# A Fourier mixer and a two-layer network on one core: transform tables in thirds, and another order of loads at the start

## The chip, the cores and the metric

The kernel runs on 1 core of one Trainium2 chip. The metric is the device time of one execution in microseconds (us), as the median of several runs. Only one core works, so its own span is the whole story. The engines are named as in the profile: PE (matrix products; PEld is its weight loading), DVE (vector), ACT (activation), POOL (GpSimd, which here only issues transfers) and SP (which also only issues transfers).

## The reference

Eight sequences of 3,008 rows and 256 columns are filtered in the frequency domain along the rows, and every row of the result goes through two dense layers with a PReLU between them. Inputs and output are float32.

```python
X = np.fft.rfft(x, axis=1)                       # x: (8, 3008, 256)
Y = X * (filt_r + 1j * filt_i)[None, :, :]       # 1505 frequencies x 256
y = np.fft.irfft(Y, n=3008, axis=1).reshape(24064, 256)
h = y @ w_in                                     # (24064, 2048)
g = np.maximum(h, 0.0) + alpha * np.minimum(h, 0.0)
out = g @ w_out                                  # (24064, 256)
```

## The kernel before

**The transform.** A transform of 3,008 = 94 x 32 points is done as matrix products: a product with a 94-point table (`wf1` or `wfx`), a reordering, a product with the twiddle table `twf`, the multiplication with the filter, a product with the inverse twiddle tables `twi` (and `twx`, for batch 0), another reordering and a product with `wi3`. Its result is the transposed activation `yT` in fp16. A twiddle table has 24 entries along its middle dimension, two for each of the 12 steps `kp` of batch 0; they can be loaded in slices such as 0:8, 8:16 and 16:24.

**Batch 0** (class `First`) has nothing to overlap with, so it is a prologue of its own, written out in order. `piece_a` (8 pieces) is the first product, `turn_at` transposes, `twice` copies a third of `twf` into a doubled form on ACT, `piece_b(kp)` is the second product followed by DVE's multiplication with the filter (line 304, output `uu`), `piece_c(kp)` is the inverse product with `twi` and `twx` (line 324, outputs named `op` or `psF`), and `keep_c` evicts it. `piece_b` writes one of two PSUM buffers called `hps`; DVE's multiplication frees it. The loop over `kp` runs `piece_b(kp + 2)`, then `piece_c(kp)`. The helper `warm` issues products whose result nobody reads.

**Loads of the prologue.** There are two queues, and each is in order. SP loads `id16`, `wfx`, the first third of `twf`, the first filter row `fst` (line 122), then at `i == 3` the rest of the tables and small constants (lines 365 and 392 to 396). GpSimd loads x of batch 0 (line 112, with conversion to fp16), filter rows 1 to 4, 4 to 8 and 8 to 12 (line 122, eight transfers each), then at `kp == 5` the layer weights `win_s` and `wout_s` (lines 422 and 424) and x of batch 1, and at last the copy of `fst` into `filt_s` (line 431) and copies within the filter (434, 436). A small `memset` by DVE into the target stands ahead of some loads: the load must wait for it, so it starts no sooner than DVE gets there. Each queue has eight completion semaphores in turn, so that a transfer also waits for the landing of the one eight places ahead of it.

**Buffers that couple things.** `fst` and `asb` (the evicted first product of batches 1 to 7, line 255 with output `asb`) have one buffer together: asb of batch 1 cannot be written before the copy of `fst` has been made. x has four buffers (`p_x`), one for each quarter of a batch.

**The main loop.** The rows go through the two layers in 48 blocks of 512 (now and then 384) rows with 16 steps each; a step is a product with `w_in` (`up`, line 481, output `hps`), ACT's eviction into `gtb` (line 490), DVE's PReLU (493 and 495), and the product with `w_out` of the block before (`down`, line 512, output `op`). The transforms of batches 1 to 7 are spread over these steps by `plan_fft`, whose arguments are step numbers: `a_at` for the first product (line 155), `x_at` for the loads of the next batch's x, `b_at` for the second product (line 179) with DVE's two multiplications (186 and 187) and the swap of partitions by transfers `uu<-ww` (line 191, GpSimd's queue), `c_at` for the inverse product (line 210). For batch 1 `b_at` is 36, 42, ..., 66 and `c_at` is 48, 54, ..., 78. For batch 2 the loads of the x that follows are at steps 57, 69, 81 and 89.

Of the kernel before, what the change touches and what calls it, by code (L numbers as in the profile page):

```python
# [24 lines left out]
def _build_consts():  # L25

    n1, n2, p = np.arange(N1), np.arange(N2), np.arange(32)
    k1 = (2 * (np.arange(NK) // 2) + 24 * (np.arange(NK) % 2))[None, :] + np.arange(2)[:, None]
    k2 = np.where(p < 16, p, 47 - p)
    g = np.where(p < 16, 1.0, -1.0)  # L30

    a1 = 2 * np.pi * n1[:, None, None] * k1[None] / N1
    wf1 = np.stack([np.cos(a1), -np.sin(a1)], axis=2)
    scale = np.where((k1 == 0) | (k1 == 47), 1.0, 2.0)[None, :, None, :] / NFFT
    wi3 = (wf1 * scale).reshape(N1, 96).T
    wfx = wf1.transpose(0, 3, 1, 2).reshape(N1, 96)
    wf1 = wf1.reshape(N1, 96)

    kk = k1[:, :, None] + N1 * k2
    ang = 2 * np.pi * n2[:, None, None, None] * kk[None] / NFFT  # L40
    c, s = np.cos(ang), np.sin(ang)
    fwd = np.array([[c, -s * g], [s, c * g]])
    twf = fwd.transpose(3, 0, 2, 4, 1, 5).reshape(128, NK, 64)
    inv = np.array([[c, s], [-s * g, c * g]])
    inv = inv.reshape(2, 2, N2, 2, NK // 2, 2, 32).transpose(5, 0, 6, 4, 3, 1, 2)
    inx = np.stack([inv[:, 1], -inv[:, 0]], axis=1)
    return wf1, wfx, wi3, twf, inv.reshape(128, NK, 64), inx.reshape(128, NK, 64)
# [3 lines left out]
def kernel(  # L51
# [10 lines left out]
    nc = tc.nc  # L62
    names = ("wf1", "wfx", "wi3", "twf", "twi", "twx")
    consts = {n: nc.inline_tensor(np.ascontiguousarray(v).astype(np.float16), name="c_" + n)
              for n, v in zip(names, _build_consts())}
    sgn = np.tile(np.repeat([1.0, -1.0], 32), 2)[:, None].astype(np.float32)
    sgn_d = nc.inline_tensor(sgn, name="c_sgn")
    id32_d = nc.inline_tensor(np.eye(16, dtype=np.float32), name="c_id32")
# [17 lines left out]
    wf1_s = konst.tile([N1, 96], FP16, name="wf1_s")  # L86
    wfx_s = konst.tile([N1, 96], FP16, name="wfx_s")
    wi3_s = konst.tile([96, N1], FP16, name="wi3_s")
    twf_s = konst.tile([128, NK, 64], FP16, name="twf_s")
    twi_s = konst.tile([128, NK, 64], FP16, name="twi_s")  # L90
    filt_s = konst.tile([128, 12, 2, D], FP16, name="filt_s")
    filts_s = konst.tile([128, 12, 2, D], FP16, name="filts_s")
    al16 = konst.tile([16, 128], FP32, name="al16")
    id32 = konst.tile([16, 16], FP32, name="id32")
# [7 lines left out]
    sgn_s = konst.tile([128, 1], FP32, name="sgn_s")  # L102
    yT = konst.tile([128, 2, 2 * NFFT], FP16, name="yT")

    def xrow(b, c):
        return bass.AP(tensor=x.tensor, offset=x.offset + (b * NFFT + 8 * c) * D,
                       ap=[[N2 * D, N1], [1, 8 * D]])

    def load_x(b, c):
        xs = p_x.tile([N1, 8 * D], FP16, name="xs")  # L110
        for r in (slice(0, 48), slice(48, N1)) :
            nc.gpsimd.dma_start(out=xs[r], in_=xrow(b, c)[r])  # L112
        return xs

    def load_filt(eng, dst, ha, hb):
        n = hb - ha
        for i, src in enumerate((filt_r, filt_i)):
            for e in range(2):
                q = 64 * e + 32 * i
                k = 2 * ha + 24 * e  # L120
                for j, step, off in ((0, 1, k), (16, -1, N1 - k)):
                    eng.dma_start(
                        out=dst[q + j : q + j + 16, ha:hb].rearrange("p h r d -> p (h r) d"),
                        in_=bass.AP(tensor=src.tensor, offset=src.offset + off * D,
                                    ap=[[N1 * D, 16], [step * D, 2 * n], [1, D]]))

    def banks(wide):
        if wide:
            return psH.tile([128, 2, 512], FP32, name="hps")
        return psF.tile([128, 2, 512], FP32, name="psF")  # L130

    def bank(kind):
        if kind == "o":
            return psO.tile([128, 2, D], FP32, name="op").rearrange("p k d -> p (k d)")
        return banks(kind == "h")[:, 0]
# [226 lines left out]
    def tables(eng, names, ka, kb):  # L362
        for n, t in (("twf", twf_s), ("twi", twi_s), ("twx", twx_s)):
            if n in names:
                eng.dma_start(out=t[:, ka:kb], in_=consts[n].ap()[:, ka:kb])

    xc = {(0, c): load_x(0, c) for c in range(4)}
# [6 lines left out]
    def warm(n, pw):  # L374
        for _ in range(n):
            nc.tensor.matmul(pw.rearrange("p (r c) -> p r c", r=4), id16,  # L376
                             id16.unsqueeze(1).to_broadcast([128, 4, 128]), start=True, stop=True)

    warm(9, bank("o"))
    for i in range(8):  # L380
        f0.piece_a(i, both[i % 2], i % 3 < 2)
        if i % 2 == 1:
            warm((4, 4, 6, 3)[i // 2], bank("o"))
        if i == 1:
            nc.vector.memset(f0.fst[:, 0, :, 0:1], 0.0)
            load_filt(nc.sync, f0.fst, 0, 1)
        if i == 3:
            nc.vector.memset(twf_s[:, 8:24, 0:1], 0.0)
            tables(nc.sync, ("twf",), 8, 24)
            tables(nc.sync, ("twi", "twx"), 0, 8)  # L390
            tables(nc.sync, ("twi", "twx"), 8, 24)
            nc.sync.dma_start(out=wi3_s, in_=consts["wi3"].ap())
            nc.sync.dma_start(out=al16, in_=moe_alpha.rearrange("(j p) -> j p", p=128))
            nc.sync.dma_start(out=id32, in_=id32_d.ap())
            nc.sync.dma_start(out=wf1_s, in_=consts["wf1"].ap())
            nc.sync.dma_start(out=sgn_s, in_=sgn_d.ap())
        if i == 5:
            f0.twice(0, 8)
    f0.turn_at(0, 1, on_act)
    f0.turn_at(1, 1, on_dve, True)  # L400
    warm(2, bank("o"))
    f0.piece_b(0)
    f0.turn_at(2, 2, on_act)
    f0.twice(8, 16)
    f0.piece_b(1)
# [3 lines left out]
    for kp in range(12):  # L409
        if kp < 10:  # L410
            f0.piece_b(kp + 2)
        f0.piece_c(kp)
        if kp > 9:
            f0.keep_c(kp, (on_act, on_act) if kp == 10 else both, 1)
        elif kp % 2 == 1:
            f0.keep_c(kp - 1, (on_act, on_act))
            if kp < 7:
                f0.turn_at(kp + 5, 2, on_act)
        if kp == 5:
            nc.vector.memset(win_s[:, 0, 0:2], 0.0)  # L420
            for kt in range(2):
                nc.gpsimd.dma_start(out=win_s[:, kt], in_=moe_w_in[kt * 128 : (kt + 1) * 128])
            for q in range(2):
                nc.gpsimd.dma_start(
                    out=wout_s[:, 8 * q : 8 * q + 8],
                    in_=moe_w_out[1024 * q : 1024 * q + 1024].rearrange("(j p) d -> p j d", p=128))
            for c in range(4):
                xc[(1, c)] = load_x(1, c)
        if 7 <= kp < 10:
            warm(2, banks(False)[:, 0])  # L430
# [92 lines left out]
    def put(step, fn, *args):  # L523
        plan.setdefault(step, []).append((fn, args))

    def plan_fft(b, a_at, ta, quarters, x_at, b_at, add, c_at, d_at):
        f = Fft(b)
        for i in range(8):
            put(a_at[i], f.piece_a, i)
            front.add(a_at[i])  # L530
        for c in range(4):
            put(a_at[2 * c + 1], f.save_a, c)
            if b + 1 < NB:
                put(x_at[c],
                    lambda b=b, c=c: xc.update({(b + 1, c): load_x(b + 1, c)}))
        for q in range(quarters):
            w = NK // quarters
            put(ta, f.turn_a, nc.sync, w * q, w * q + w)
        for q in range(6):
            put(b_at[q], f.piece_b, q, not add)  # L540
            if add:
                put(b_at[q] + add, f.piece_s, q)
        for q in range(6):
            put(c_at[q], f.piece_c, q)
            front.add(c_at[q])
            if q % 2 == 1:
                put(c_at[q] + 1, f.turn_c, q // 2)
        for i in range(8):
            put(d_at[i], f.pair_d, i, on_act)
# [13 lines left out]
    def d_steps(p):  # L563
        return [p + t for t in (91, 93, 104, 108, 116, 120, 140, 152)]

    plan_fft(1, range(12, 28, 2), 28, 4, (34, 42, 54, 66), range(36, 72, 6), 0, range(48, 84, 6),
             (92, 94, 97, 100, 111, 121, 142, 154))
    plan_fft(2, (50, 56, 62, 68, 74, 80, 82, 84), 90, 4, (57, 69, 81, 89),
             (106, 116, 126, 136, 148, 158), 7, (116, 126, 136, 148, 158, 172), d_steps(96))
    for b in range(3, NB):  # L570
        p = 96 * (b - 1)
# [54 lines left out]
```

## Time and profile before

| | |
|---|---|
| median of 3 runs | 790.9 us (789.08 to 791.35) |
| the profiled execution | 787.85 us, its span 786.0 us |
| mean granted PE clock | 0.993 |
| PE busy | 769.7 us (98% of the span) |
| DVE, ACT busy | 595.5 us (76%), 587.0 us (75%) |
| chain that ended last | PE 92%, DMA 4% |
| transfers | 100.66 MB, SP's queue 34.1% and GpSimd's 21.5% of 16 engines |

The chain is the sequence of work, followed back from the last instruction, that set the end. A share of 98% for PE says that nearly all of the span is PE's, but not at which clock, and matrix products overlap, so that a busy PE is not one at its peak. The first 60 us, in which batch 0 is transformed and the loop fills, look otherwise than the rest: there PE waits, and there the granted clock is 0.50 in two stretches.

### The profile page before, as it was taken

The page shows a single profiled execution, that of the slowest core. Times are in us where ns is not written, and L with a number is a line of the kernel's source. Part 1 is how long each engine was busy: PE and PEld are TensorE (multiplying, and loading weights), DVE is VectorE, ACT ScalarE, POOL GpSimd, SP SyncE. Part 2 cuts the span into 40 slices and gives each one's busy share as a digit, 9 for nine tenths or more (in the row PEclk, how much of TensorE's full clock was granted, in tenths as well). Part 3 has the DMA queues.
Part 4 walks back from the last instruction along what each step waited for, and adds up shares of the span by engine and source line. Part 5 has one row for each costly group of instructions (what it writes and reads, how often), then busy time and mean ns, then how long its engine had stood idle before and what let it go on. Part 6 is the DMA issues. An engine that isn't in the chain of part 4 may idle for free.

```text
span 786.0 us, 16085 instructions
## 1 busy us (share of the span) xinstructions
PE 769.7 (98%) x6349; PEld 511.8 (65%) x6349; DVE 595.5 (76%) x1116; ACT 587.0 (75%) x673; POOL 142.7 (18%) x271
## 2 busy tenths in 40 slices
PE   7889999999999999999999999999999999999997
PEld 4547666666666666766666666766666666766665
DVE  3668885788868887788877888688877888766663
ACT  4578787887778887798777887788876777677663
POOL 6420471122202221122201222011200121000000
PEclk9899999999999999999999999999999999999999
DMA  9897698766754657455593655734474233511112
GB/s 188 133 180 203 125 185 181 234 136 161 144 156 109 146 136 148 135 123 126 128 216 73 148 124 130 189 82 108 109 154 129 57 86 93 147 38 28 42 41 55
DMA packets 95084, 100.66 MB, mean 128 GB/s; under 512 B 11280, under 2 KB 82464, under 8 KB 94816
## 3 DMA queue, kind: packets, MB, share of 16 engines
q1 hardware_dynamic: 80368, 70.25, 34.1%
q0 software_dynamic: 14640, 29.38, 21.5%
q8 instruction: 50, 0.82, 0.4%
q14 instruction: 26, 0.21, 0.1%
HBM read 55.28 MB, written 46.66 MB: 130 GB/s over the span
## 4 chain that ended last, share of the span: by engine, by line
PE 92%; DMA 4%; issue 1%; POOL 1%; ACT 1%; DVE 1%; POOLq 0%; ACTq 0%; DVEq 0%
PE op L512 41%; PE hps L481 41%; PE hps L155 3%; PE psF L232 3%; DMA filt_s<-in_filt_r_dram 2%; PE psF L179 2%; PE hps L210 1%; DMA uu<-ww 1%; DMA filt_s<-fst 1%; POOL xs L112 1%; PE psF L346 0%; PE op L324 0%; ACT gtb L490 0%; PE hps L299 0%; PE psF L376 0%
## 5 line engine op out<-in xcount | busy, mean ns | idle before, releaser
L490 ACT ACTIVATE gtb<-hps 128x1024 f16<-128x1024 f32 (+1 forms) x384 | 385.8, 1005 | 133.2 <-PE hps L481 132.3
L512 PE MATMUL op<-wout_s,gtb 128*128 128x256 f16 x3008 | 436.3, 273 | 0.1
L481 PE MATMUL hps<-yT,win_s 128*128 128x512 f16 (+1 forms) x1536 | 434.8, 375 | 1.2 <-ACT gtb L490 1.1
L512 PEld LDWEIGHTS <-gtb 128*128 128x128 f16 x3008 | 294.0, 98 | 168.9 <-issue 0.9
L493 DVE TENSOR_SCALAR m<-gtb,alm_s 128x512 f16<-128x512 f16 (+1 forms) x768 | 233.0, 346 | 150.7 <-ACT gtb L490 149.7
L495 DVE TENSOR_TENSOR gtb<-gtb,m 128x2048 f16<-128x2048 f16 (+1 forms) x192 | 231.0, 1203 | 10.4 <-PE hps L481 0.5
L481 PEld LDWEIGHTS <-win_s 128*128 128x128 f16 x1536 | 142.8, 98 | 61.5 <-issue 15.4
L193 POOL DMA_DIRECT2D sw<-ww x144 | 71.1, 501 | 380.7 <-DVE ww L186 377.8
L255 ACT ACTIVATE asb<-hps 96x1024 f16<-96x1024 f32 x56 | 57.1, 1020 | 13.1 <-PE hps L155 11.7
L517 ACT ACTIVATE osb<-op 128x512 f32<-128x512 f32 (+1 forms) x97 | 56.2, 579 | 5.3 <-issue 2.8
L255 ACT ACTIVATE v<-hps 128x1024 f16<-128x1024 f32 x42 | 43.0, 1025 | 15.7 <-PE hps L210 15.7
L112 POOL DMA_DIRECT2D xs<-in_x_dram x64 | 39.1, 700 | 85.6 <-PE hps L155 73.9
L255 ACT ACTIVATE yT<-psF 128x752 f16<-128x752 f32 x59 | 47.0, 797 | 7.8 <-PE psF L232 7.7
L186 DVE TENSOR_TENSOR ww<-psF,filts_s 128x1024 f16<-128x1024 f32 x42 | 51.1, 1218 | 0.0
L187 DVE TENSOR_TENSOR uu<-psF,filt_s 128x1024 f16<-128x1024 f32 x42 | 51.0, 1215 | 0.0
L155 PE MATMUL hps<-xs,wf_s 94*96 94x512 f16 x112 | 33.9, 384 | 1.4 <-ACT asb L255 1.4
L232 PE MATMUL psF<-wi_s,zt 96*128 96x94 f16 x500 | 31.2, 205 | 0.2
L232 PEld LDWEIGHTS <-zt 96*128 96x128 f16 x512 | 28.6, 98 | 2.9 <-issue 0.6
L191 POOL DMA_DIRECT2D uu<-ww x24 | 19.3, 1208 | 31.6 <-DVE uu L187 26.4
L198 DVE TENSOR_TENSOR uu<-uu,sw 128x1024 f16<-128x1024 f16 x36 | 24.7, 685 | 0.3 <-DMA sw<-ww 0.3
L210 PE MATMUL hps<-uu,twi_s 64*64 64x256 f16 x336 | 16.8, 271 | 1.1 <-DMA uu<-ww 1.1
L179 PE MATMUL psF<-at,twf_s 64*64 64x256 f16 x336 | 17.3, 281 | 0.0
(67 smaller groups left out, 173.2 us busy)
## 6 DMA issues: line engine op xcount, KB each, us to landing
out_dram<-osb SPq DMA_DIRECT2D x160, 128.0 KB
a_dram<-asb SPq DMA_DIRECT2D x28, 384.0 KB
v_dram<-v SPq DMA_DIRECT2D x84, 128.0 KB
zt<-v_dram SPq DMA_DIRECT2D x28, 384.0 KB
sw<-ww POOLq DMA_DIRECT2D x144, 64.0 KB, 2.4
at<-a_dram SPq DMA_DIRECT2D x20, 384.0 KB
xs<-in_x_dram POOLq DMA_DIRECT2D x32, 192.0 KB, 4.5
xs<-in_x_dram POOLq DMA_DIRECT2D x32, 184.0 KB, 5.8
```

Source lines behind the costliest of these rows:

```text
L155: nc.tensor.matmul(ps[0:96, u], wf1_s, xs[:, o : o + 512], start=True, stop=True)
L186: nc.vector.tensor_mul(ww, px, fs)
L187: nc.vector.tensor_mul(uu, px, f)
L193: nc.gpsimd.dma_start(out=sw[o : o + 32], in_=ww[i : i + 32])
L232: nc.tensor.matmul(ps[:, m], self.zt[:, 8 * g + 4 * mh + m, dh * 128 : dh * 128 + 128], wi3_s, start=True, stop=True)
L255: nc.scalar.activation(o, i, AF.Copy)
L481: nc.tensor.matmul(self.hps[:, j % 2, 0:tn], win_s[:, kt, j * 128 : (j + 1) * 128], yT[:, kt, self.t0 : self.t0 + tn], start=(kt == 0), st ...
L490: nc.scalar.activation(g[:, 2 * i : 2 * i + 2], self.hps[:, :, 0:tn], AF.Copy)
L493: nc.vector.tensor_scalar(m[:, 2 * i + h], g[:, 2 * i + h], 0.0, a, OP.min, OP.mult)
L495: nc.vector.tensor_add(g, g, m)
L512: nc.tensor.matmul(self.op[:, si - s0], self.gts[k][:, 128 * si : 128 * si + 128], wout_s[:, k], start=(si == s0 and k == 0), stop=(si == ...
L517: nc.scalar.activation(osb[:, 0:m], self.op[:, 0:m], AF.Copy)
```

## The change

The tables come in thirds. At `i == 3` SP now loads the second third of `twf`, the first third of `twi` and `twx`, and the last third of `twf`. The second and last thirds of `twi` and `twx`, and the small constants behind them, are issued behind `piece_b(0)`, with a DVE memset ahead of them that holds them until the first filter multiplication is done. The memset and the loads of the layer weights go from `kp == 5` to `kp == 4`, and the first quarter of x of batch 1 goes between `w_in` and `w_out`. The loads of x of batch 2 are put at steps 32, 40, 50 and 58 instead of 34, 42, 54 and 66. In GpSimd's queue this last edit changes one place: the last of these four quarters (two transfers) now stands ahead of the four swaps of the fifth `piece_b` of batch 1, not behind them. The number of matrix products, evictions and filter multiplications is the same.

```diff
         if i == 3:
-            nc.vector.memset(twf_s[:, 8:24, 0:1], 0.0)
-            tables(nc.sync, ("twf",), 8, 24)
+            nc.vector.memset(twf_s[:, 8:16, 0:1], 0.0)
+            tables(nc.sync, ("twf",), 8, 16)
             tables(nc.sync, ("twi", "twx"), 0, 8)
-            tables(nc.sync, ("twi", "twx"), 8, 24)
-            nc.sync.dma_start(out=wi3_s, in_=consts["wi3"].ap())
-            nc.sync.dma_start(out=al16, in_=moe_alpha.rearrange("(j p) -> j p", p=128))
-            nc.sync.dma_start(out=id32, in_=id32_d.ap())
-            nc.sync.dma_start(out=wf1_s, in_=consts["wf1"].ap())
-            nc.sync.dma_start(out=sgn_s, in_=sgn_d.ap())
+            tables(nc.sync, ("twf",), 16, 24)
...
     f0.piece_b(0)
+    nc.vector.memset(twi_s[:, 8:16, 0:1], 0.0)
+    tables(nc.sync, ("twi", "twx"), 8, 16)
+    tables(nc.sync, ("twi", "twx"), 16, 24)
+    nc.sync.dma_start(out=wi3_s, in_=consts["wi3"].ap())
+    nc.sync.dma_start(out=al16, in_=moe_alpha.rearrange("(j p) -> j p", p=128))
+    nc.sync.dma_start(out=id32, in_=id32_d.ap())
+    nc.sync.dma_start(out=wf1_s, in_=consts["wf1"].ap())
+    nc.sync.dma_start(out=sgn_s, in_=sgn_d.ap())
...
-        if kp == 5:
+        if kp == 4:
             nc.vector.memset(win_s[:, 0, 0:2], 0.0)
             for kt in range(2):
                 nc.gpsimd.dma_start(out=win_s[:, kt], in_=moe_w_in[kt * 128 : (kt + 1) * 128])
+            xc[(1, 0)] = load_x(1, 0)
             for q in range(2):
                 nc.gpsimd.dma_start(
                     out=wout_s[:, 8 * q : 8 * q + 8],
                     in_=moe_w_out[1024 * q : 1024 * q + 1024].rearrange("(j p) d -> p j d", p=128))
-            for c in range(4):
+            for c in range(1, 4):
                 xc[(1, c)] = load_x(1, c)
...
-    plan_fft(1, range(12, 28, 2), 28, 4, (34, 42, 54, 66), range(36, 72, 6), 0, range(48, 84, 6),
+    plan_fft(1, range(12, 28, 2), 28, 4, (32, 40, 50, 58), range(36, 72, 6), 0, range(48, 84, 6),
              (92, 94, 97, 100, 111, 121, 142, 154))
```

## The prediction

> **What bounds the kernel now.** I read the whole-span table first: PE is busy 769.7 of 786.0 us, so apart from its clock only about 16 us can be had, all of it where PE waits. The list of who waited for whom, over the first 90 us, says where.
>
> ```profile
> DVE uu L304 <- DMA filt_s<-in_filt_r_dram: 2.4, 1, 2.4
> PE hps L299 <- DVE uu L304: 2.0, 2, 1.7
> PE hps L155 <- ACT asb L255: 1.4, 1, 1.4
> ```
>
> PE stands twice, both times behind somebody else's wait: DVE's first multiply with the second third of the filter (kp = 4), and ACT's first eviction of batch 1 into asb. The chain that ended last shows what released those two.
>
> ```profile
> 21.28 2.37 DMA filt_s<-in_filt_r_dram
> 23.65 0.04 DVE uu L304
> ...
> 44.02 6.36 DMA filt_s<-fst
> 50.38 0.66 issue
> 51.04 0.04 ACTq L255
> ```
>
> The second needs a word: asb and fst share one buffer (tag "asb"), so ACT may not write asb before the copy of fst into filt_s has landed. That copy is the last of GpSimd's queue of layer weights and x. Stage windows of 3.41 us, laid on the edges of the granted clock, show what each wait costs besides (columns: length; PE, PEld, DVE, ACT, POOL busy; clock; DMA share; GB/s).
>
> ```profile
> 18.92:22.33 3.41, 2.68 (x83) 1.76 (x76) 2.28 (x2) 3.41 (x5) 1.01 (x2) 1.00 1.09 178
> 22.33:25.74 3.41, 1.67 (x52) 1.32 (x49) 2.11 (x2) 2.15 (x4) 2.55 (x5) 1.00 0.84 115
> 25.74:29.15 3.41, 3.11 (x56) 2.05 (x55) 2.86 (x5) 1.89 (x3) 0.58 (x2) 0.50 0.17 19
> 29.15:32.56 3.41, 3.41 (x57) 1.54 (x52) 2.57 (x3) 1.20 (x3) 3.41 (x6) 0.50 0.79 120
> 49.63:53.04 3.41, 1.68 (x7) 0.63 (x6) 3.14 (x6) 2.67 (x5) 1.78 (x4) 1.00 0.31 64
> 53.04:56.45 3.41, 3.34 (x10) 1.53 (x10) 0.94 (x4) 1.95 (x3) 0.17 (x1) 0.50 0.93 205
> ```
>
> A window with PE busy 1.67 or 1.68 us (49%) is followed by half clock; one with 2.68 us (79%) is not. Where the edge lies between is not shown.
>
> **Part 1, the tables.** Before, five SP transfers (1,024 KB) are issued from 13.09 to 15.4 us, beside the eight of GpSimd for filter rows 4 to 8 (issued 13.42 to 17.4). From 15 to 21 us the DMA view gives SP's queue 1.04 MB and 58.1% of the engines, GpSimd's 0.52 MB and 56.7%: full. From 24 to 26 us, alone, GpSimd's queue moves 0.25 MB at 97.4%. The change leaves 512 KB in the early batch and sends 512 KB (half of 58.1% of 6 us: 1.75 us of engines) from behind the first multiply. That ends at 16.22 + 1.23 = 17.45; the new DVE memset (0.07 us as at L388) follows, SP issues from 17.5, and data moves a good microsecond later (the first load: issued 0.74, used 2.54). So there is a gap of some 1.5 us, from about 17.3 to 18.8, in which the filter has the engines alone; afterwards the tables come back and share them. Bounds: 0 (the engines stay full, and what is deferred returns before the filter's last packets) and -1.75 (it all falls behind). I take -0.5: in the gap the filter gains about 0.5 to 0.6 of 1.5 us, and loses a part again after 18.8. DVE's wait is 2.44 us, so all of it counts on PE's chain.
>
> What could turn late: the second third of twx and twi is first used by piece_c(4), at 25.26; issued by 18.4, it has 6.8 us, where a table of this size issued at 13.96 was in use at 18.72. The last third is needed at 31.89, wi3 at 38.84, alpha at 40.03, wf1 at 49.09. The last twf third now stands fourth in SP's queue, with 512 KB up to its end; ACT needs it at 19.54, and before, the table that ended 512 KB was used at 18.72. Three more SP issues (0.32 to 0.44 us) cost nothing, as SP's next entry is at 53.99. The memset lies ahead of the second multiply, on a DVE that waits 2.44 us soon after. All zero; if the cover fails, piece_c(4) waits and the gain goes.
>
> **Part 2, layer weights and x.** DVE's memset of win_s, which releases GpSimd, moves ahead of the eighth multiply: four take 4.62 us, so 1.15 us sooner, 1.65 with part 1; the first weight load goes out at 26.9 instead of 28.57. The DMA moves nothing from 27 to 29 us before, so nothing is displaced. From 30 to 49 us GpSimd's queue alone moves 3.66 MB at 113%: bytes set the end, and the same bytes begin 1.65 us sooner. So fst lands near 48.7, not 50.38. ACT is free for asb at 49.59 + 0.79 = 50.38, 0.5 sooner after part 1: asb begins at 49.9 instead of 51.12. Its row shows the 0.74 us of idle that goes:
>
> ```profile
> 51.12 1.02 ACT L255 ACTIVATE asb<-hps 96x1024 f16<-96x1024 f32 x1 [0.74 <-PE hps L481]
> ```
>
> I take -0.7 (bounds 0, if something else holds the copy, and -0.74). What is late next is ACT itself: PE still waits some 0.7 us for asb to leave the first of two hps buffers. x of batch one ahead of wout: 384 KB at 195 GB/s put wout back 2.0 us, less the 1.65; it had landed by 43.19 and is needed at 54.77. Nothing.
>
> The second half-clock window: with asb 1.2 us sooner, PE does in the 3.41 us before 53.04 the rest of four L481 (0.64), two L155 (0.60), four L481 (1.02) and a beginning L512 (0.14): 2.4 us, 70%. That lies nearer 79% than 49%, so I take it as kept at full clock. In 53.04 to 56.45 PE did 3.34 us of work that takes 1.67 at full clock; ACT, with 1.0 us in each of its two evictions per pair of products, gives back some 0.4. So -1.3, bounds 0 and -1.67. The first such window goes from 1.67 to 2.17 us, 64%: between the rows, and I leave it cold.
>
> The Trainium skill ("TensorE: Matmul & The Clock Gate", section "Why this matters for your kernels") says that only PE-idle gaps above about 3 us take the clock back. By it neither window above would have been half clock, and the -1.3 would be 0, for a sum of -0.7; the trace does not agree, as gaps of 1.4 to 2.0 us, with a window 51% idle, were followed by 0.50.
>
> **Part 3, x of batch 2 at steps 32, 40, 50, 58.** GpSimd's queue is in order and its entries go when their data is ready, so steps matter only by order. One pair changes: the last quarter of x (384 KB) now stands ahead of the swaps uu<-ww of piece_b(4) instead of behind them. The landing records before give: x of batch 3 at 113.49, these swaps at 116.40 (used by piece_c(4) at 117.27), the x quarter at 119.08, the swaps of piece_b(5) at 124.77. The last is a wait now:
>
> ```profile
> PE hps L210 <- DMA uu<-ww: 1.1, 1, 1.1
> ```
>
> From 113 to 120 us both queues together take 99.7% of the engines. With x ahead, the swaps of piece_b(4) land up to 119.08 - 116.40 = 2.7 us later: 119.1, so piece_c(4) waits up to 1.8. The bytes ahead of piece_b(5)'s swaps are the same, so they land as before, and its 1.05 us wait is swallowed: +0.8. At best x uses idle engine time and +0, or the 1.05 goes: -1.05. At worst both stand: +1.8. I take +0.5, nearer the upper rows as the engines are full.
>
> **Sum:** -0.5 - 0.7 - 1.3 + 0.5 = -2.0 us. The profiled execution took 787.85 us (span 786.0 and 1.85 around it): 785.85. It is 3.05 below the median of the runs, 790.9 (spread 789.08 to 791.35), and the same difference there gives 788.9. Under 0.3%, 2.4 us, a measurement of this kernel cannot tell from no change; the forecast lies just inside.
>
> **Rivals.**
> 1. The first stretch stays warm too (64% suffices). DVE, at 1.16 us a multiply, then bounds kp = 4 to 11: 8 x 1.16 from 23.1 ends at 32.4, not 34.7, 2.3 us sooner. But fst still lands near 48.7 and ACT would be free at 48.1, so asb waits again, for 0.6: a gain of 1.8 up to there in place of 1.2, -2.6 in all, -4.1 if the x quarter also takes the 1.05 us away. For: 64% is well above 49%. Against: the clock stayed 0.50 even after a window with 3.11 us busy.
> 2. The clock gives nothing back: 70% busy does not suffice, and the second window stays at half clock. Then -0.5 - 0.7 + 0.5 = -0.7, 790.2; if the tables gain nothing either, -0.2, 790.7. For: engines full from 15 to 21 us, and the edge is unknown between 49% and 79%. Against: 70% is the nearer to 79%. The Trainium skill's page named above comes to the same sum by its rule.
> 3. Slower: the x quarter. If the swaps lose the full 2.7 us, PE stands 1.8 us at piece_c(4), and where one clock window holds all of that (47% busy, under the 49% above) half clock follows, at 1.7. Place: PE at 117; price 3.5 - 1.05 = +2.45 with the gains of part 2 small (-0.7): +1.8, 792.7; with none, 793.3. It decides from 0.87 us of delay on, the slack between 116.40 and 117.27. Against: x of batch 3 lands ahead in any case, and the step could let x slip into a lull.
> 4. The change does not do what it says: GpSimd is held by some landing rather than by the memset, so that the weights leave as late as before. Against: the filter's transfers are all in by 27 us. Then -0.5 + 0.5 = 0.
>
> **How the numbers follow.** Forecast 0.42 (788.9; its own range 787.3 to 789.9, for the x quarter from -1.05 to +1.5), first rival 0.20 (786.8 to 788.3), second 0.18 (790.2), slower 0.13 (792.7), fourth 0.07 (790.9). Faster by over 0.3% (under 788.5): the first rival and two fifths of the forecast, 0.37. Slower by over 0.3% (over 793.3): the half of the third rival that has no gain beside it, and 0.09 for a wait moved elsewhere in a start where each wait hides the next: 0.16. The rest, 0.47, is within. The range goes from the first rival, 786.8, less half of the spread of the runs (1.1), to the third with no gain beside it: 785.7 to 793.3.
>
> **What would show it.** Right: the first L304 of kp = 4 begins near 23.1, not 23.63; win_s loads near 26.9; fst into filt_s landed by 49; ACT's asb with no idle before it; clock 1.00 after 53 us; L210 waiting near 117 and no more near 124. Wrong: L304 unmoved (the tables did not matter); L324 waiting for twi_s or gtb; win_s issued with no DVE wait before it; half clock after 53 us though asb came early (the 70% does not suffice); no wait at L210 (x slipped through), or one above 2 us with half clock behind it.

## The result, and the profile after

The change made the kernel faster: 784.58 us median (783.33 to 786.87) against 791.23 us, ratio 0.9925 with a 95% interval of 0.9904 to 0.9946. Run again twice beside the experiments, each time on a chip with before, it gave 786.40 against 789.60 us (0.9953, 0.9931 to 0.9976) and 784.72 against 788.95 us (0.9944, 0.9924 to 0.9965). By medians that is 6.65, 3.2 and 4.2 us; pooled, the spans average 787.5 us in the 102 runs of before that stood beside the experiments and 783.4 us in all 27 of the change, 4.1 us. The forecast was 2.0.

The profiled execution of the change took 786.87 us (span 784.8), the longest of its six, and that of before 787.85 us, below all six of its runs. So the two profiles differ by 1.0 us only: they are read here for where the waits stand, and the sizes come from the many runs. Who waited for whom, in the first 90 us of the change:

```profile
PE op L324 <- ACT v L255: 2.9, 4, 2.1
PE hps L155 <- ACT asb L255: 2.0, 1, 2.0
ACT gtb L255 <- DMA twf_s<-c_twf: 1.6, 1, 1.6
DVE uu L304 <- DMA filt_s<-in_filt_r_dram: 1.2, 1, 1.2
```

DVE's wait for the filter has halved, PE no longer waits for DVE at kp = 4, but a new wait has come: ACT for the last third of `twf`, and PE behind ACT (line 324). At asb PE waits longer than before, 2.0 us for 1.4. The rows of DVE and ACT give the times. First DVE's filter multiplies from kp = 4 on (four in one row in before) and the memset that releases the layer weights, before and after.

```profile
23.63 4.62 DVE L304 TENSOR_TENSOR uu<-hps,filt_s 128x1024 f16<-128x1024 f32 x4 [2.44 <-DMA filt_s<-in_filt_r_dram]
28.20 0.06 DVE L420 MEMSET win_s<- 128x1 uint32 x1
```

```profile
22.52 1.22 DVE L304 TENSOR_TENSOR uu<-hps,filt_s 128x1024 f16<-128x1024 f32 x1 [1.21 <-DMA filt_s<-in_filt_r_dram]
26.63 0.06 DVE L423 MEMSET win_s<- 128x1 uint32 x1
```

Then ACT, for the last third of `twf` (before, then after) and for asb (after).

```profile
19.54 1.05 ACT L255 ACTIVATE gtb<-twf_s 128x1024 f16<-128x1024 f16 x1
```

```profile
21.36 1.06 ACT L255 ACTIVATE gtb<-twf_s 128x1024 f16<-128x1024 f16 x1 [1.60 <-DMA twf_s<-c_twf]
```

```profile
49.71 1.02 ACT L255 ACTIVATE asb<-hps 96x1024 f16<-96x1024 f32 x1 [1.31 <-DVE m L497]
```

The filter multiply of kp = 4 starts at 22.52 (23.63 before), asb at 49.71 (51.12). ACT's 1.31 us of idle is put down to DVE's line 497, but that had nothing to give it: the copy of `fst` landed at 49.56. GpSimd's row for the next entry, which waits for the same copy, says so, in before (where the row merges four entries) and in the change:

```profile
51.26 1.96 POOL L434 DMA_DIRECT2D filts_s<-filt_s  x4 [6.66 <-DMA filt_s<-fst]
```

```profile
49.84 0.50 POOL L438 DMA_DIRECT2D filts_s<-filt_s  x1 [8.44 <-DMA filt_s<-fst]
```

In before the copy landed at 50.98, by the same records, and asb started at 51.12. So the copy already ended ACT's wait there, and 50.38, which the prediction took for the landing, is the time at which ACT's previous eviction ended. In all fifteen profiles with the copy at its old place, asb starts 0.14 to 0.15 us after the landing.

Stage windows on the edges of the change's own clock (columns as before):

```profile
18.54:21.95 3.41, 2.28 (x65) 1.50 (x65) 2.77 (x3) 1.81 (x3) 0.65 (x3) 1.00 1.11 227
21.95:25.36 3.41, 2.11 (x57) 1.41 (x57) 2.36 (x2) 3.17 (x6) 2.45 (x5) 1.00 0.90 142
25.36:28.77 3.41, 3.13 (x96) 2.06 (x94) 3.10 (x5) 3.17 (x5) 1.77 (x4) 1.00 0.44 44
49.26:52.67 3.41, 1.57 (x8) 0.71 (x8) 2.13 (x5) 2.84 (x3) 1.95 (x4) 1.00 0.57 115
52.67:56.09 3.42, 3.42 (x13) 1.58 (x11) 1.84 (x3) 2.04 (x2) 0.00 (x0) 0.50 1.00 241
```

The first wait, 2.13 us of PE from 20.82 to 22.95, is parted by the edge at 21.95, so that both windows stay above 60%. A window with PE busy 2.11 us (62%) was followed by full clock, one with 1.57 us (46%) by half. So the stretch after the first wait is now at full clock, and the one after the second is not: the other way round than forecast.

### The profile page after: what moved, and what is told of

It is laid out like the page before. It is cut to its first block, busy times and chain, and to the rows that moved or that the text cites. A ratio compares the mean times of both kernels' runs of the same rounds, so it can differ in the third digit from the quotient of the medians.

```text
span 784.8 us, 16091 instructions
## 1 busy us (share of the span) xinstructions
PE 768.7 (98%) x6349; PEld 511.6 (65%) x6349; DVE 595.2 (76%) x1117; ACT 587.3 (75%) x673; POOL 142.6 (18%) x271
## 4 chain that ended last, share of the span: by engine, by line
PE 92%; DMA 3%; DVE 2%; ACT 2%; issue 1%; POOL 0%; SPq 0%; ACTq 0%; DVEq 0%; POOLq 0%
PE hps L485 41%; PE op L516 41%; PE hps L155 3%; PE psF L232 3%; PE psF L179 2%; PE hps L210 1%; DMA uu<-ww 1%; DMA twf_s<-c_twf 1%; ACT v L255 1%; ACT gtb L494 1%; DMA xs<-in_x_dram 1%; PE psF L346 1%; DMA fst<-in_filt_r_dram 1%; DVE m L497 1%; PE op L324 0%
## 5 line engine op out<-in xcount | busy, mean ns | idle before, releaser
L112 POOL DMA_DIRECT2D xs<-in_x_dram x64 | 37.3, 672 | 82.6 <-PE hps L155 74.3
L186 DVE TENSOR_TENSOR ww<-psF,filts_s 128x1024 f16<-128x1024 f32 x42 | 51.1, 1217 | 0.0
```

The source lines that it names most:

```text
L186: nc.vector.tensor_mul(ww, px, fs)
```

## The experiments

Two theories were tested first. "Clock": the gain is the half clock that no longer follows the first wait. "Loads": it is the earlier end of GpSimd's queue. In the table, the ratio is to before on the same chip with its 95% interval, "kp = 4" is the start of DVE's filter multiply of kp = 4 in the run's profile, "asb" that of ACT's first asb, and the clock is the mean over all runs.

| kernel | median, us (before) | ratio | kp = 4 | asb | clock |
|---|---|---|---|---|---|
| e1_tables | 786.49 (789.08) | 0.9969 (0.9949 to 0.9989) | 21.81 | 48.81 | 0.9967 |
| e2_loads | 787.59 (789.08) | 0.9979 (0.9959 to 0.9999) | 24.48 | 50.90 | 0.9961 |
| e3_xat | 788.81 (789.08) | 1.0000 (0.9985 to 1.0015) | 23.98 | 50.95 | 0.9955 |
| e4_fill | 788.49 (789.08) | 0.9992 (0.9978 to 1.0007) | 24.00 | 51.12 | 0.9970 |
| a0_after | 786.40 (789.60) | 0.9953 (0.9931 to 0.9976) | 21.54 | 48.51 | 0.9970 |
| a1_noxat | 786.20 (789.60) | 0.9957 (0.9935 to 0.9979) | 21.23 | 47.70 | 0.9982 |
| a2_twf | 786.16 (789.60) | 0.9945 (0.9923 to 0.9967) | 21.92 | 48.55 | 0.9968 |
| a3_fst | 783.31 (789.60) | 0.9914 (0.9889 to 0.9938) | 21.92 | 47.31 | 0.9985 |
| b1_nohold | 786.10 (789.02) | 0.9945 (0.9926 to 0.9964) | 23.20 | 49.73 | 0.9976 |
| b2_kp5 | 787.42 (789.02) | 0.9959 (0.9936 to 0.9981) | 21.13 | 48.71 | 0.9962 |
| b3_xlast | 784.57 (789.02) | 0.9927 (0.9904 to 0.9951) | 21.92 | 49.26 | 0.9973 |
| b4_before_fst | 787.17 (789.02) | 0.9971 (0.9951 to 0.9991) | 24.56 | 50.68 | 0.9967 |
| c0_after | 784.72 (788.95) | 0.9944 (0.9924 to 0.9965) | 21.82 | 48.56 | 0.9975 |
| c1_nohold | 786.19 (788.95) | 0.9953 (0.9933 to 0.9973) | 23.42 | 49.73 | 0.9970 |
| c2_fill | 784.20 (788.95) | 0.9929 (0.9904 to 0.9954) | 21.54 | 48.31 | 0.9990 |
| c3_fst_nohold | 784.10 (788.95) | 0.9926 (0.9902 to 0.9949) | 24.21 | 49.37 | 0.9982 |

The mean clock of before is 0.9951 over its 102 runs.

### The parts one at a time

**e1_tables**: before with the tables' edits alone.

```diff
-            tables(nc.sync, ("twf",), 8, 24)
+            tables(nc.sync, ("twf",), 8, 16)
             tables(nc.sync, ("twi", "twx"), 0, 8)
-            tables(nc.sync, ("twi", "twx"), 8, 24)
+            tables(nc.sync, ("twf",), 16, 24)
...
     f0.piece_b(0)
+    nc.vector.memset(twi_s[:, 8:16, 0:1], 0.0)
+    tables(nc.sync, ("twi", "twx"), 8, 16)
+    tables(nc.sync, ("twi", "twx"), 16, 24)
```

> Only part 1: tables in thirds, inverse thirds behind the first multiply; loads of layer weights and x as before. Theory 'clock': the first filter multiply of kp = 4 starts about 1 us sooner, the window with PE's wait is no longer followed by 0.50, and of the 6.65 us this part alone gives 3 to 5. Theory 'loads' (the gain lies in the earlier end of GpSimd's queue): this part alone gives 0.5 to 1.5, since the copy of fst into filt_s lands hardly sooner and ACT waits for it all the longer.

It gave 2.6 us by the medians, and its profile runs at full clock from 7.9 us to 782.7 us, just short of its end. But asb comes at 48.81 though the loads' order is the old one: the earlier multiply carried GpSimd's queue with it, and ACT waited 1.6 us for the copy. Neither theory alone fits. How the queues share the engines shows why the filter came sooner. First before, then e1_tables, both from 16 to 19 us (q1 is SP's queue, q0 GpSimd's; packets, MB, share of 16 engines):

```profile
q1 hardware_dynamic: 480, 0.64, 69.1%
q0 software_dynamic: 210, 0.15, 35.8%
```

```profile
q0 software_dynamic: 435, 0.32, 77.3%
q1 hardware_dynamic: 309, 0.28, 30.3%
```

In these three microseconds the filter's queue moves 0.32 MB in place of 0.15. The other profiles agree: its share there is 33% to 45% in the five with the old tables, 48% to 55% in the three with thirds but no hold (b1_nohold, c1_nohold, c3_fst_nohold), and 58% to 80% in the ten with the hold.

**e2_loads**: before with the layer weights at `kp == 4` and the first quarter of x between `w_in` and `w_out`.

```diff
-        if kp == 5:
+        if kp == 4:
...
+            xc[(1, 0)] = load_x(1, 0)
```

> Only part 2: layer weights at kp = 4, x of batch one between w_in and w_out; tables as before. Theory 'clock': PE's wait at kp = 4 and the half clock after it stay, asb comes 0.7 us sooner; 1 to 2 us gained. Theory 'loads': 3 to 5 us gained.

1.5 us by the medians, as theory "clock" had it, and hardly clear of its interval; its profile keeps half clock from 25.17 to 31.99 us. But asb comes only 0.2 us sooner than in before there, not 0.7: in this profile the multiply of kp = 4 is late (24.48), and the first load leaves at 28.29 in place of 28.57. That profile is of one of the longest runs of the twelve (790.48 us).

**e3_xat**: before with x of batch 2 at steps 32, 40, 50, 58.

```diff
-    plan_fft(1, ..., 4, (34, 42, 54, 66), ...
+    plan_fft(1, ..., 4, (32, 40, 50, 58), ...
```

> Only part 3: loads of x of batch 2 at steps 32, 40, 50, 58. Both theories: within 1.5 us of before; the prediction's +0.5, from a wait of up to 1.8 us at piece_c(4) in place of the 1.05 us at piece_c(5).

No difference. The mechanism is there: PE waits at piece_c(4), from 117.0 us, and no more at piece_c(5).

```profile
PE hps L210 <- DMA uu<-ww: 1.4, 2, 0.9
```

That is 1.42 us in place of 1.05, a term of +0.4, though one profile says little here: this wait is between nothing and 1.05 us in the six profiles without the edit and between nothing and 1.7 us in the twelve with it. Some of it may come back: three of the six profiles without the edit (e1_tables, e2_loads, b4_before_fst) show line 232 waiting 1.2 to 2.0 us between 133 and 138 us for the reload `zt<-v_dram`; of the twelve with it, one does (c2_fill, 1.2). No run isolates this.

**e4_fill**: before with seven idle products in PE's first wait.

```diff
+        if kp == 4:
+            warm(7, bank("o"))
         if kp < 10:
             f0.piece_b(kp + 2)
```

> Before, with seven idle products (warm) put into PE's wait ahead of piece_b(6); no load is moved. They start when ACT has freed the buffer, about 23.3 us, and last 1.5 us, inside the wait that ends at 24.9. Theory 'clock': the window goes from 49% to over 90% busy, no half clock from 25.7 us on, 1.5 to 3 us gained though no wait is shorter. Theory 'loads': no gain, since the copy of fst into filt_s ends ACT's wait at the same time.

The clock stays full through the first wait, and DVE's last multiply of batch 0 starts at 31.94 us in place of 33.47. Yet asb still starts at 51.12, to the hundredth as in before, with its idle grown from 0.74 to 2.31 us:

```profile
51.12 1.02 ACT L255 ACTIVATE asb<-hps 96x1024 f16<-96x1024 f32 x1 [2.31 <-issue]
```

and half clock follows there instead, from 51.51 to 58.34 us. The whole gained 0.6 us, not clear of its interval. So theory "clock" falls as a cause by itself: what is won before 50 us is lost in the second wait unless GpSimd's queue starts sooner as well.

### One chain: start of the queue, copy of fst, asb

From the issue of the first weight load to the start of asb it is 22.55 us in before and 22.71 in the change, and between 21.8 and 23.2 in all fifteen profiles that have the copy of `fst` at its old place. The next five kernels bear on that.

**a0_after**: the change as it is.

> The changed kernel as it is, beside the others on one chip. Theory 'both': the two parts at the start are one chain, so the whole gives more than part 1 alone (2.6 us) and part 2 alone (1.5 us): 4 to 6 us below before, with a mean granted clock near 0.998 against 0.995. Theory 'clock alone': as part 1 alone, 2.5 to 3.5 us.

3.2 us by medians, 3.6 by means: under the 4 to 6 of theory 'both', and by the medians in the range of 'clock alone'; the mean clock is 0.9970, not 0.998. So this run does not decide between them. The parts alone gave 2.6 and 1.5 us on another chip; their sum, 4.1, is the pooled gain of the change, but the scatter of the comparisons (3.2 to 6.65) is too wide to show that they add up.

**a3_fst**: the change with the copy moved.

```diff
             xc[(1, 0)] = load_x(1, 0)
+            nc.gpsimd.dma_start(out=filt_s[:, 0:1], in_=f0.fst)
...
-    nc.gpsimd.dma_start(out=filt_s[:, 0:1], in_=f0.fst)
```

> The change with the copy of fst into filt_s moved ahead of w_out in GpSimd's queue. Theory 'the queue sets the second wait': the copy lands about 10 us sooner, ACT's first asb no longer waits (1.3 us in the change), the clock stays at 1.00 after 52 us, and the whole is 2 to 3 us faster than the change. Rival 'ACT is the limit there': PE's wait shrinks by no more than the 1.3 us and half clock still follows, under 1.3 us gained.

3.1 us faster than the change on the same chip by medians (2.6 by means, clear of the scatter), 6.3 below before. The copy lands at 37.13. ACT goes to asb without idle, PE's wait at line 155 is 0.57 us, and the profile has full clock to 780.4 us, 0.2 us before its end:

```profile
46.63 0.79 ACT L255 ACTIVATE yT<-psF 128x752 f16<-128x752 f32 x1
47.31 1.02 ACT L255 ACTIVATE asb<-hps 96x1024 f16<-96x1024 f32 x1
```

So the queue set the second wait of the change. This version beats both kernels.

**b4_before_fst**: before with the same move.

> Before, with only the copy of fst moved ahead of w_out. Theory 'one chain, two waits': the first wait (kp = 4) stays, the second goes: asb 0.7 us sooner and no half clock behind it, 1 to 2.5 us below before, clearly less than the 3 us which the same move gave to the change, where ACT came to the copy earlier. Rival 'only the second wait matters': as fast as the change with the copy moved, 6 us below before.

1.85 us, inside the first theory's range; asb at 50.68 without idle of ACT (0.4 us sooner, not 0.7, with a late kp = 4), full clock behind it, with half clock still after the first wait (25.27 to 32.09 us). With the first wait still there the move gives less than the 3.1 us that it gave to the change, though the intervals overlap.

**b2_kp5**: the change with the layer weights at `kp == 5` again.

```diff
-        if kp == 4:
+        if kp == 5:
```

> The change with the layer weights back at kp = 5. Theory 'the queue sets the second wait': everything in GpSimd's queue goes 1.15 us later, asb too: 1 to 2 us slower than the change. Rival 'ACT sets it': no difference.

1.6 us below before where the change stands at 3.2 and 4.2 on other chips: the side that was expected, but not beyond the intervals. On its own chip it is 2.9 us slower than b3_xlast, the next kernel, which is the change but for the order of x. Its one profile does not show why: asb comes at 48.71, no later than in the change (48.51 to 49.71), since kp = 4 is the earliest of all there, and the first load leaves 5.2 us after it and not 4.0 as in a0_after.

**b3_xlast**: the change with the first quarter of x behind `w_out`.

```diff
-            xc[(1, 0)] = load_x(1, 0)
...
-            for c in range(1, 4):
+            for c in range(4):
```

> The change with the first quarter of x of batch 1 behind w_out again. Both theories: the bytes ahead of the copy of fst are the same, so no difference from the change within 0.5 us; if x ahead mattered, line 155 would now wait for xs at about 47 us.

4.45 us below before, like the change: this edit is worth nothing that can be measured.

### The tables: thirds, hold, order

**b1_nohold**, and again as **c1_nohold** beside the change: no memset, the inverse tables issued at once.

```diff
             tables(nc.sync, ("twf",), 16, 24)
+            tables(nc.sync, ("twi", "twx"), 8, 16)
+            tables(nc.sync, ("twi", "twx"), 16, 24)
...
-    nc.vector.memset(twi_s[:, 8:16, 0:1], 0.0)
-    tables(nc.sync, ("twi", "twx"), 8, 16)
-    tables(nc.sync, ("twi", "twx"), 16, 24)
```

> The change without the hold: the tables in thirds and in the new order, but the inverse second and last thirds issued at once, not behind the first multiply. Theory 'holding them back frees the filter': the first multiply of kp = 4 begins 1 to 2 us later than in the change, near 23, and 1 to 2.5 us of the whole go. Rival 'thirds suffice' (smaller packets let the filter in between): no difference from the change.

> The change without the hold once more, now beside the change. Theory 'the start of GpSimd's queue decides': the hold brings the start of the layer weights 1 to 1.5 us forward, so without it 1 to 1.5 us slower than the change. Rival 'what the hold brings is lost again in the second wait': no difference within 0.5 us.

**c0_after**: the change, beside it.

> The changed kernel once more, on the chip of the three that follow: 3 to 6 us below before, as in the two comparisons so far (6.65 and 3.2 by their medians).

The hold does to the filter what was expected and more. The multiply of kp = 4 starts at 23.63 to 24.56 us in the five profiles with the old tables (mean 24.1), at 23.20 to 24.21 in the three with thirds and no hold (23.6), and at 21.13 to 22.52 in the ten with it (21.7): 0.5 us for the thirds, 1.9 for the hold. Each of these starts is from one profile. Half clock set in between 21 and 26 us in four of the five (the fifth is e4_fill), in two of the three, and in none of the ten. In those two it follows another wait than DVE's: PE stands at line 324, behind ACT or the load of `twx`, from 20.76 to 22.0 us in b1_nohold and from 18.68 to 20.13 us in c3_fst_nohold, where half clock begins at 21.09. In the whole time the hold shows less: 1.5 us between c1_nohold and c0_after by medians, 0.9 by means; b1_nohold is not slower than the change on other chips by its ratio, but 1.5 us by medians and 1.2 by means slower than b3_xlast on its own chip. All of it lies inside the scatter.

**c3_fst_nohold**: a3_fst without the hold, so that the second wait covers nothing.

> The change with the copy of fst moved ahead of w_out (a3_fst) and without the hold. With the second wait gone, what the first multiply loses is no longer covered: theory 'the hold is worth what its wait is, once the queue does not bind' gives 1.5 to 3 us more than a3_fst, so 3 to 5 us below before where a3_fst stood 6 below. Rival 'the hold is worth nothing': as a3_fst.

4.85 us below before where a3_fst stood 6.3 below on another chip: the low end of the first theory, and again inside the intervals. The three comparisons point the same way, but what the hold is worth in the whole, between nothing and some 2 us, stays open.

**a2_twf**: the change with the last third of `twf` ahead of the first inverse thirds.

```diff
-            tables(nc.sync, ("twi", "twx"), 0, 8)
             tables(nc.sync, ("twf",), 16, 24)
+            tables(nc.sync, ("twi", "twx"), 0, 8)
```

> The change with the last third of twf ahead of the first third of twi and twx in SP's queue. The profile of the change shows ACT waiting 1.6 us for that third and PE 2.1 us behind ACT at 21 us. If that wait counts, the first multiply of kp = 5 comes about 0.5 us sooner and the whole is 0.3 to 1 us faster than the change; the rival, that piece_c(0) waits for twx instead or that ACT's wait for the copy of fst swallows it, gives no difference.

No difference. In its profile ACT is served sooner (the third `twice` at 19.22; 21.36, 19.85 and 20.39 in the three profiles of the change, so that the wait of 1.60 us is not in each of them), but asb, at 48.55, is where it was in a0_after: the rival.

**a1_noxat**: the change without its last edit.

```diff
-    plan_fft(1, ..., 4, (32, 40, 50, 58), ...
+    plan_fft(1, ..., 4, (34, 42, 54, 66), ...
```

> The change without its last edit (x of batch 2 at steps 34, 42, 54, 66 as before). The prediction's term: 0.5 us faster than the change, the wait at piece_c(4) gone and one at piece_c(5) back. Rival: the edit pays elsewhere (the reload of zt of batch 1, for which line 232 waited 1.2 and 2.0 us at 134 us in the runs without it), then 0.5 to 2 us slower than the change.

No difference from the change, and no wait at line 210 in its profile: as in e3_xat, neither theory's number.

### The half clock behind the second wait

**c2_fill**: the change with eight idle products in the second wait.

```diff
+    put(14, lambda: warm(8, bank("o")))
     plan_fft(1, range(12, 28, 2), ...
```

> The change with eight idle products at step 14, inside PE's second wait (2.0 us in the change's profile); no load is moved and no wait is shorter. Theory 'half clock is part of the price of the second wait': mean granted clock from 0.997 to 0.9985 or more, 0.7 to 1.5 us faster than the change. Rival 'only the wait itself costs': no difference.

The clock does what was expected: 0.9990 against 0.9975 in c0_after. The window with the wait is 82% busy and the next one at full clock:

```profile
49.12:52.53 3.41, 2.78 (x15) 1.26 (x13) 1.24 (x4) 3.15 (x5) 1.28 (x3) 1.00 1.01 202
52.53:55.94 3.41, 3.41 (x25) 2.40 (x25) 2.40 (x5) 2.86 (x3) 0.49 (x1) 1.00 0.92 227
```

The time is 0.5 us lower than c0_after's by medians and 0.9 by means, not clear of the scatter, so that the price of the half clock is not shown by this run. In the many runs a low clock and a long span go together: among the 102 of before, those at clock 0.9975 or above average a span of 785.6 us, those at 0.994 or below 789.0, and a line through all of them gives 650 us per unit of mean clock, 1.4 us for each stretch of 3.41 us (correlation 0.68). This is no proof of a cause: a run with a longer wait can have both the lower clock and the longer span.

## Why the prediction was wrong, step by step

The direction was right, the place right, and the size wrong: 2.0 us forecast, 4.1 pooled (6.65 in the first comparison, 3.2 and 4.2 in the two others), with the first result, 784.58 us, just under the range, the third, 784.72, too, and the second, 786.40, inside it. The first comparison is the widest of the three partly by chance: its six runs of before have a median of 791.23, against 788.95 to 789.60 on the four chips of the experiments.

- **Tables, -0.5 forecast: mis-sized, and this is the step that failed.** The tables' edits alone gave 2.6 us (e1_tables). The multiply of kp = 4 comes 1.1 us sooner in the change's profile, 2.4 on the average of the profiles with and without the edit. The working let the filter gain in a gap of 1.5 us and give part of it back after 18.8. The queue views show what it missed: already from 16 to 19 us the filter's share of the engines doubles (35.8% to 77.3%), and the thirds alone do part of it (51.2% in c1_nohold). By the average of 2.4 the bound of 1.75 was too near as well.
- **"The last twf third ... all zero": wrong in the profile.** The third landed at 21.34, not about 18.7, and ACT waited 1.60 us. It cost nothing that can be measured in the whole, as a2_twf shows; that the second wait swallowed it is the likely reason.
- **The first window left cold, the second warm: both wrong, for one reason.** With the larger shift the first two windows were 67% and 62% busy, and that suffices. Then ACT was free for asb at 48.40 and not 49.9, sooner than the copy could land, waited 1.31 us, and the second window was 46% busy and not 70%. That 70% would have kept the clock full was right: every window of 58% or more did (last section). This is the mechanism of the first rival, which was given 0.20. It put asb 1.8 us sooner; in the three profiles of the change it is 1.4, 2.6 and 2.6. It also kept the second window warm, and in those profiles it is half clock. The 1.3 us that the sum took for the clock is near the 1.4 us that the many runs suggest, but by luck: the sum saved the stretch behind the second wait, and in the profiles the one behind the first is gone.
- **Layer weights, -0.7 at asb: right in mechanism, and it carries more.** The first load left at 27.00 (26.9 forecast). The landing near 48.7 was 49.56. Its base was misread: the copy landed at 50.98 in before and not at 50.38, and 50.98 less the 1.65 is 49.33. So the copy, and not ACT, still ended the wait at asb. The term should have been the whole shift of the queue's start, as asb follows it by 22 to 23 us. The loads' edits alone gave 1.5 us (e2_loads).
- **x of batch 2, +0.5:** the wait for the swaps moved from piece_c(5) to piece_c(4) as forecast, 0.83 us in the change's profile for 1.05, with another 0.70 at line 210 put down to ACT; in the whole no cost can be measured (e3_xat, a1_noxat).
- **x ahead of wout, nothing:** right (b3_xlast).

Worked again from the runs, as an estimate: asb 2.2 us sooner (48.9, the mean of three profiles of the change, against 51.1 in the one of before), and a mean clock of 0.9974 for 0.9951, which at the smaller slope of the change's own runs, 600 us per unit, is 1.4: 3.6 of the 4.1 us. The two terms may count some time twice, as the mean clock also holds the stretch behind the first wait, which lies ahead of asb and whose removal alone gave nothing clear (e4_fill). So the direct evidence is that of the parts and of a3_fst, and how the 4.1 us divide between waits and clock stays open.

## What to carry to other kernels

When a transfer that holds a chain shares the engines with another queue, count what the other queue takes in the microseconds where the chain's transfer is served: deferring by a few microseconds what is needed later brought the filter 1.9 us forward in the profiles, beside 0.5 for the thirds, where the sum took 0.5 for both. Two waits in a row are one chain when a queue's start hangs on the first and its end releases the second. What is gained between them without an earlier start of the queue is lost again in the second (e4_fill); an earlier start moves both (e1_tables), and moving the thing that the second waits for frees it (a3_fst). And one profile is one draw: here the profile of before was shorter than all six runs of the first comparison, that of the change was the longest of its six, and only many runs told the size.

## What the runs showed of the hardware

The half clock comes in stretches of 3.41 us or twice that, on edges that lie differently in each run. A window with PE busy 49% or less (1.57, 1.67, 1.68 us) was followed by half clock, one with 62% or more (2.11, 2.78 us) by full, in the windows shown. Laid on the edges of each run's own clock, the windows of all 18 profiles up to the last stretch bear it out and narrow it: all fifteen at full clock with PE busy up to 1.87 us (55%, b1_nohold) were followed by half, all with 1.99 us or more (58%, a1_noxat) by full, and of the three between, 1.96 us in c3_fst_nohold was followed by half, 1.89 us in a2_twf and 1.96 us in e1_tables by full. Whole gaps of PE of 1.42, 1.99 and 3.0 us sufficed for it at the second wait (before, the change, e4_fill), and a gap of 2.28 us in e1_tables, which an edge parts, passed without, so that the place of the edges decides. (In before the two gaps are 1.67 and 1.42 us; the 2.0 us in the prediction is the total of two waits.) The Trainium skill ("TensorE: Matmul & The Clock Gate", section "Why this matters for your kernels") asks for gaps above about 3 us; the measurements here differ.
